# First loads on one queue and a held transposing load, in a gated attention and SwiGLU kernel

## Chip, cores, metric

One core of one Trainium2 chip. The metric is the device time of one execution in microseconds (us), median of several runs. All runs quoted here are undisturbed ("fast").

## The reference, cut

```python
def reference(A_x, A_wqkv, A_wo, B_x, B_w1, B_w3, B_w2, gate_w):
    x = A_x                                   # 1 x 2048 x 512, bf16
    g = sigmoid((x * gate_w).sum(-1, keepdims=True))
    # a: linear attention, 32 heads of 16; phi(t) = where(t > 0, t + 1, exp(t)) + 1e-6
    #    q, k, v from x @ wqkv; kv = phi(k)^T v; z = sum of phi(k); (phi(q) kv) / (phi(q) z) @ wo
    # b: (silu(x @ w1) * (x @ w3)) @ w2, hidden size 1376
    return g * a + (1 - g) * b
```

## The kernel before

Only the head matters: the first 10 us, in which TensorE (PE) warms up on constants, then transposes the first four token tiles of x itself and multiplies them with wk, while the rest of x arrives by transposing loads. PE's order is fixed by hand.

```python
dq = nc.sync
x_pairs = x2d[0:TB, :].rearrange("(g p j) d -> g p j d", p=P, j=2)      # TB = 512, P = 128
dq.dma_start(out=x_sb[:, 0:2, :], in_=x_pairs[0])                                   # "x pair 0"
nc.scalar.dma_start(out=wk_sb[:, 0:2, :], in_=wqkv_r[:, 0:2, D : 2 * D])            # "wk half 0"
dq.dma_start(out=wk_sb[:, 2:4, :], in_=wqkv_r[:, 2:4, D : 2 * D])                   # "wk half 1"
dq.dma_start(out=x_sb[:, 2:TPB, :], in_=x_pairs[1])                                 # "x pair 1"
pre = consts.tile([1, 1], FP32, name="pre")
nc.scalar.activation(out=pre[:], in_=..., func=ACT.Exp)     # loads the table early
for tb in range(1, NTB):
    dq.dma_start(out=xT[:, :, tb * TB : (tb + 1) * TB],     # transposing load
                 in_=x2d[tb * TB : (tb + 1) * TB, :], transpose=True)
    dq.dma_start(out=x_sb[:, tb * TPB : (tb + 1) * TPB, :], in_=x_r[:, ...])
# ... all other weights on dq; two Pool memsets of hr (128x512), 
# ... then PE in program order:
emit_warm(TB, TB, TB, TB, TB, TB, P, P, P)    # matmuls on constants
emit_xT(0); emit_xT(1)                        # PE transposes of x pair 0, copied to xT by DVE and ACT
for kc, t in ((0, 0), (1, 0), (0, 1), (1, 1), (2, 0), (3, 0)):   # four with wk half 0, two with half 1
    emit_k_mm(k0[t], t, kc)
emit_xT(2); emit_xT(3)                        # needs x pair 1
# ... ten more k matmuls, then per token tile t from 4: XP matmuls of tile t-4, k matmuls of tile t
#     (the first reader of a transposing load is token tile 4)
```

Of the kernel before, what the change touches and what calls it, by code (L numbers as in the profile page):

```python
# [11 lines left out]
ENG = mybir.EngineType  # L12
FP32 = mybir.dt.float32
BF16 = mybir.dt.bfloat16
# [3 lines left out]
def kernel(  # L18
# [12 lines left out]
    nc = tc.nc  # L31
    P = nc.NUM_PARTITIONS

    Bb, S, D = A_x.shape
    F = B_w1.shape[1]
# [3 lines left out]
    NT = S // P  # L39
    TB = 512  # L40
    NTB = S // TB
    TPB = TB // P
    FC = F // P
    FR = F - FC * P
    FM = FC * P
    NR = 2 * FR + 1
    HPC = P // Dh

    x2d = A_x.flatten_outer_dims()
    out2d = out.flatten_outer_dims()  # L50

    consts = ctx.enter_context(tc.tile_pool(name="consts", bufs=1))
# [11 lines left out]
    x_sb = consts.tile([P, NT, D], BF16, name="x_sb")  # L64
    xT = consts.tile([P, KC, S], BF16, name="xT")
    wk_sb = consts.tile([P, KC, D], BF16, name="wk_sb")
    wq_sb = consts.tile([P, KC, D], BF16, name="wq_sb")
    wv_sb = consts.tile([P, KC, D], BF16, name="wv_sb")
    w1_sb = consts.tile([P, KC, FM], BF16, name="w1_sb")
    w3_sb = consts.tile([P, KC, FM], BF16, name="w3_sb")  # L70
    wr_sb = consts.tile([P, KC, NR], BF16, name="wr_sb")
    w2_sb = consts.tile([P, FC, D], BF16, name="w2_sb")
    w2r_sb = consts.tile([P, D], BF16, name="w2r_sb")
    wo_sb = consts.tile([P, KC, D], BF16, name="wo_sb")

    wqkv_r = A_wqkv.rearrange("(kc d) n -> d kc n", d=P)
    w1_r = B_w1.rearrange("(kc d) f -> d kc f", d=P)
    w3_r = B_w3.rearrange("(kc d) f -> d kc f", d=P)
    x_r = x2d.rearrange("(t p) d -> p t d", p=P)
    dq = nc.sync  # L80
    x_pairs = x2d[0:TB, :].rearrange("(g p j) d -> g p j d", p=P, j=2)
    out_pairs = out2d[0:TB, :].rearrange("(g p j) d -> g j p d", p=P, j=2)
    dq.dma_start(out=x_sb[:, 0:2, :], in_=x_pairs[0])
    nc.scalar.dma_start(out=wk_sb[:, 0:2, :], in_=wqkv_r[:, 0:2, D : 2 * D])
    dq.dma_start(out=wk_sb[:, 2:4, :], in_=wqkv_r[:, 2:4, D : 2 * D])
    dq.dma_start(out=x_sb[:, 2:TPB, :], in_=x_pairs[1])
    pre = consts.tile([1, 1], FP32, name="pre")
    nc.scalar.activation(out=pre[:], in_=nc.const_aps.tensor(0.0, [1, 1], FP32), func=ACT.Exp)
    for tb in range(1, NTB):
        dq.dma_start(  # L90
            out=xT[:, :, tb * TB : (tb + 1) * TB], in_=x2d[tb * TB : (tb + 1) * TB, :],
            transpose=True,
        )
        dq.dma_start(
            out=x_sb[:, tb * TPB : (tb + 1) * TPB, :], in_=x_r[:, tb * TPB : (tb + 1) * TPB, :]
        )
    dq.dma_start(out=wq_sb[:], in_=wqkv_r[:, :, 0:D])
    dq.dma_start(out=wr_sb[:, :, 0:FR], in_=w1_r[:, :, FM:F])
    dq.dma_start(out=wr_sb[:, :, FR : 2 * FR], in_=w3_r[:, :, FM:F])
    with nc.allow_non_contiguous_dma(reason="one gate weight per partition and chunk"):  # L100
        dq.dma_start(
            out=wr_sb[:, :, 2 * FR : NR], in_=gate_w.rearrange("(kc d o) -> d kc o", d=P, o=1)
        )
    dq.dma_start(out=wv_sb[:], in_=wqkv_r[:, :, 2 * D : 3 * D])
    for fsl in (slice(0, FM // 2), slice(FM // 2, FM)):
        dq.dma_start(out=w1_sb[:, :, fsl], in_=w1_r[:, :, fsl])
        dq.dma_start(out=w3_sb[:, :, fsl], in_=w3_r[:, :, fsl])
    dq.dma_start(out=wo_sb[:], in_=A_wo.rearrange("(kc d) n -> d kc n", d=P))
    w2_r = B_w2[0:FM, :].rearrange("(fc f) d -> f fc d", f=P)
    for fcs in (slice(0, FC // 2), slice(FC // 2, FC)):  # L110
        dq.dma_start(out=w2_sb[:, fcs, :], in_=w2_r[:, fcs, :])
    dq.dma_start(out=w2r_sb[:FR, :], in_=B_w2[FM:F, :])

    pk_sb = consts.tile([P, NT, D], BF16, name="pk_sb")
    pks = consts.tile([P, D], FP32, name="pks")
    blockmask = consts.tile([P, P], FP32, name="blockmask")
    bm = blockmask[:].rearrange("p (b j) -> p b j", j=Dh)
    nc.gpsimd.memset(blockmask[:], 1.0)
# [1 line left out]
        out=bm, in_=bm, pattern=[[-Dh, HPC], [0, Dh]], compare_op=ALU.is_ge, fill=0.0,  # L120
# [3 lines left out]
        out=bm, in_=bm, pattern=[[Dh, HPC], [0, Dh]], compare_op=ALU.is_ge, fill=0.0,  # L124
        base=Dh - 1, channel_multiplier=-1,
    )
    XP_sb = consts.tile([P, KC, D], BF16, name="XP_sb")
    kvT_sb = consts.tile([P, KC, P], BF16, name="kvT_sb")
    W_sb = consts.tile([P, KC, D], BF16, name="W_sb")
    z_sb = consts.tile([P, D], FP32, name="z_sb")  # L130
    omg = consts.tile([P, NT], FP32, name="omg")
    hr_bufs = []
    for i in range(2):
        hrb = consts.tile([P, TPB, P], BF16, name=f"hr{i}")
        nc.gpsimd.memset(hrb[:], 0.0)
        hr_bufs.append(hrb)

    def phi(dst, ps):
        e = work.tile([P, D], BF16, tag="phi_e", name="phi_e")
        e_ins = nc.scalar.activation(out=e[:], in_=ps, func=ACT.Exp)  # L140
        em = work.tile([P, D], BF16, tag="phi_m", name="phi_m")
        nc.vector.tensor_scalar(  # L142
            out=em[:], in0=e[:], scalar1=1.0, scalar2=1e-6, op0=ALU.min, op1=ALU.add
        )
        nc.vector.scalar_tensor_tensor(  # L145
            out=dst, in0=ps, scalar=0.0, in1=em[:], op0=ALU.max, op1=ALU.add
        )
        return e_ins
# [259 lines left out]
    for c in range(KC):  # L408
# [7 lines left out]
        out=kvT_sb[:], in0=kvT_ps[:],  # L416
# [70 lines left out]
```

## Time and profile before

| | before |
|---|---|
| time, median of the first 3 runs | 180.26 us (180.18 to 180.34) |
| span of the profiled run | 178.7 us |
| PE busy | 97% |
| PE's share of the chain that ended last | 97% |

The page, its busy times by engine and its chain that ended last:

```profile
PE 174.1 (97%) x877; PEld 84.6 (47%) x893; DVE 119.3 (67%) x205; ACT 66.6 (37%) x126; POOL 61.3 (34%) x69
...
PE 97%; issue 1%; DVE 0%; DVEq 0%
```

PE is the bound, and nearly everything that ended late was PE itself. The head of PE, from the timeline (start us, duration us, engine, line, operation, out<-in, shape, count; a bracket names an idle time and what ended it):

```profile
0.84 3.04 PE L161 MATMUL warm<-const-bfloat16-1.0 128*128 128x512 bf16 x9 [0.84 <-PEq L471]
3.68 1.05 PE L174 MATMUL xTp<-ident,x_sb 128*128 128x128 bf16 x8
4.53 2.01 PE L184 MATMUL k<-wk_sb,xT 128*128 128x512 bf16 x6
6.37 0.61 PE L174 MATMUL xTp<-ident,x_sb 128*128 128x128 bf16 x8
6.82 2.32 PE L184 MATMUL k<-wk_sb,xT 128*128 128x512 bf16 x10
8.98 1.03 PE L204 MATMUL XP<-pk_sb,x_sb 128*128 128x512 bf16 x4
9.84 1.03 PE L184 MATMUL k_ps<-wk_sb,xT 128*128 128x512 bf16 x4
```

No bracket after the first line: PE never sits idle in this stretch. The first eight transposes start 0.11 us apart and the second eight 0.055, so somewhere in the six k matmuls PE's pace doubles. The Trainium skill (TensorE: Matmul & The Clock Gate, Part 1) gives 106.7 ns for the cold and 55.6 ns for the warm array at 128 columns; the trace agrees. The trace's record of the granted clock puts this **release** at 5.63 us. (The page's clock row shows full speed from the start, because it has no record for the time before the first release. The pace of the matmuls is what to read.)

The loads, from SyncE's (SP's) timeline, and then x pair 1 by its source line:

```profile
0.80 0.39 SPq L83 DMA_DIRECT2D x_sb<-in_A_x_dram  x1
1.26 0.41 SPq L85 DMA_DIRECT2D wk_sb<-in_A_wqkv_dram  x1
1.72 0.46 SPq L86 DMA_DIRECT2D x_sb<-in_A_x_dram  x1
2.23 3.49 SPq L90 DMA_TRANSPOSE xT<-in_A_x_dram  x1
```

```profile
L86 SPq DMA_DIRECT2D x_sb<-in_A_x_dram x1: 459/459/459, 1.7 to 1.7; - x1
...
DMA to landing us min/median/max: 4.2/4.2/4.2
```

The second number of a load's row is the time that SP takes to issue it. x pair 1 is issued at 1.72 us and has landed 4.2 us later, at 5.95; PE's second transposes started at 6.37. That is a slack of 0.4 us.

### The profile page before, as it was taken

What the parts mean: (1) busy time and instruction counts of PE and PEld (TensorE: products, weight loads), DVE (VectorE), ACT (ScalarE), POOL (GpSimd) and SP (SyncE); (2) the same over time, 40 slices, a digit from 0 to 9 for tenths busy, and PEclk for the clock granted to TensorE, in tenths of its full rate; (3) what the DMA queues carried; (4) which work ended last, traced back from release to release, by engine and by line L of the source; (5) the groups of instructions that cost most, each with busy time, mean ns of one, the idle gap of its engine ahead of it and who ended that gap; (6) DMA issues with size and microseconds to landing.
All of it is one profiled execution on the core that took longest, in us unless ns stands there. A gap on an engine that the chain in (4) does not pass through costs nothing.

```text
span 178.7 us, 2472 instructions
## 1 busy us (share of the span) xinstructions
PE 174.1 (97%) x877; PEld 84.6 (47%) x893; DVE 119.3 (67%) x205; ACT 66.6 (37%) x126; POOL 61.3 (34%) x69
## 2 busy tenths in 40 slices
PE   8999999999999999999999999999999999999993
PEld 4444444474444545444454544444545444444463
DVE  1588867997998837398786375978754669776000
ACT  3642323476533333342433333342433323341221
POOL 5187575736353323262003232620032328100000
PEclk9999999999999999999999999999999999999999
DMA  5999999901005010124000111240001023300011
GB/s 178 263 272 245 267 321 369 321 6 28 9 12 107 0 48 29 44 55 92 0 4 6 38 37 37 59 93 2 0 7 59 14 62 64 61 0 0 29 44 50
DMA packets 29085, 14.88 MB, mean 83 GB/s; under 512 B 19632, under 2 KB 28816, under 8 KB 29072
## 3 DMA queue, kind: packets, MB, share of 16 engines
q1 hardware_dynamic: 28800, 14.46, 30.2%
q10 hardware_dynamic: 272, 0.26, 0.5%
q8 instruction: 7, 0.11, 0.3%
q14 instruction: 6, 0.05, 0.1%
HBM read 8.42 MB, written 2.10 MB: 59 GB/s over the span
## 4 chain that ended last, share of the span: by engine, by line
PE 97%; issue 1%; DVE 0%; DVEq 0%
PE o_ps L355 19%; PE gate_ps L310 19%; PE up_ps L318 19%; PE o_ps L346 8%; PE q_ps L217 8%; PE XP L204 8%; PE k_ps L184 6%; PE r_ps L241 3%; PE k L184 2%; PE o_ps L350 2%; PE warm L161 2%; PE xTp L174 1%; PE kvT_ps L411 1%; PE W_ps L438 0%; DVE o_out L364 0%
## 5 line engine op out<-in xcount | busy, mean ns | idle before, releaser
L310 PE MATMUL gate_ps<-xT,w_sb 128*128 128x512 bf16 x156 | 40.7, 379 | 0.2
L318 PE MATMUL up_ps<-xT,w_sb 128*128 128x512 bf16 x156 | 40.5, 379 | 0.2
L225 POOL TENSOR_TENSOR qz<-pq,z_sb 128x512 f32<-128x512 bf16 x16 | 18.5, 1165 | 60.3 <-DVE pq L145 58.4
L323 ACT ACTIVATE th<-gate_ps 128x512 bf16<-128x512 f32 x40 | 23.9, 597 | 38.1 <-PE gate_ps L310 36.6
L355 PE MATMUL o_ps<-w_sb,hT 128*128 128x512 bf16 (+2 forms) x176 | 37.3, 354 | 0.2
L325 DVE SCALAR_TENSOR_TENSOR gs<-th,gate_ps 128x512 bf16<-128x512 bf16 x40 | 27.3, 684 | 5.8 <-ACT th L323 5.3
L328 DVE TENSOR_TENSOR hT<-up_ps,gs 128x512 bf16<-128x512 f32 x40 | 27.6, 691 | 3.8
L142 DVE TENSOR_SCALAR phi_m<-phi_e 128x512 bf16<-128x512 bf16 x32 | 15.2, 475 | 18.9 <-ACT phi_e L140 18.8
L355 PEld LDWEIGHTS <-hT 128*128 128x128 bf16 x180 | 16.8, 97 | 17.9
L318 PEld LDWEIGHTS <-w_sb 128*128 128x128 bf16 x160 | 15.6, 98 | 18.9
L310 PEld LDWEIGHTS <-w_sb 128*128 128x128 bf16 x160 | 15.6, 98 | 18.7
L360 ACT ACTIVATE o_out<-o_ps,omg 128x512 bf16<-128x512 f32 (+2 forms) x17 | 11.2, 656 | 30.4 <-PE o_ps L355 30.4
L290 POOL TENSOR_TENSOR pqn<-pq,rden 128x512 bf16<-128x512 bf16 x16 | 16.6, 1057 | 14.0 <-DVE rden L283 11.7
L194 POOL TENSOR_TENSOR pks<-pks,pk_sb 128x512 f32<-128x512 f32 x15 | 17.3, 1155 | 8.1 <-DVE pk_sb L145 7.5
L228 DVE TENSOR_REDUCE den<-qz 128x32 f32<-128x512 f32 x16 | 11.0, 684 | 9.0 <-POOL qz L225 8.9
L346 PE MATMUL o_ps<-W_sb,pqT 128*128 128x512 bf16 (+2 forms) x71 | 16.5, 355 | 0.1
L217 PE MATMUL q_ps<-wq_sb,xT 128*128 128x512 bf16 x63 | 16.4, 379 | 0.1
L204 PE MATMUL XP<-pk_sb,x_sb 128*128 128x512 bf16 x62 | 16.0, 379 | 0.1
L140 ACT ACTIVATE phi_e<-k_ps 128x512 bf16<-128x512 f32 x12 | 7.2, 597 | 14.4 <-PE k_ps L184 12.2
L140 ACT ACTIVATE phi_e<-q_ps 128x512 bf16<-128x512 f32 x16 | 9.6, 597 | 7.8 <-PE q_ps L217 6.7
L184 PE MATMUL k_ps<-wk_sb,xT 128*128 128x512 bf16 x48 | 12.3, 379 | 0.1
L145 DVE SCALAR_TENSOR_TENSOR pq<-q_ps,phi_m 128x512 bf16<-128x512 f32 x16 | 11.1, 691 | 0.5
(59 smaller groups left out, 119.5 us busy)
## 6 DMA issues: line engine op xcount, KB each, us to landing
w_sb<-in_B_w_dram SPq DMA_DIRECT2D x6, 640.0 KB, 8.5
out_dram<-o_out SPq DMA_DIRECT2D x15, 128.0 KB, 1.7
x_sb<-in_A_x_dram SPq DMA_DIRECT2D x3, 512.0 KB, 4.4
x_sb<-in_A_x_dram SPq DMA_DIRECT2D x2, 256.0 KB, 3.5
wq_sb<-in_A_wqkv_dram SPq DMA_DIRECT2D x1, 512.0 KB, 6.6
wv_sb<-in_A_wqkv_dram SPq DMA_DIRECT2D x1, 512.0 KB, 6.5
wo_sb<-in_A_wo_dram SPq DMA_DIRECT2D x1, 512.0 KB, 9.5
wk_sb<-in_A_wqkv_dram ACTq DMA_DIRECT2D x1, 256.0 KB, 3.7
```

The costliest lines, as they stand in the source:

```text
L184: nc.tensor.matmul(k_ps[:], lhsT=xT[:, kc, t * P : (t + 1) * P], rhs=wk_sb[:, kc, :], start=(kc == 0), stop=(kc == KC - 1),)
L194: nc.gpsimd.tensor_add(pks[:], pks[:], pk_sb[:, t, :])
L204: nc.tensor.matmul(XP_ps[dc][:], lhsT=x_sb[:, t, dc * P : (dc + 1) * P], rhs=pk_sb[:, t, :], start=(t == 0), stop=(t == NT - 1),)
L217: nc.tensor.matmul(q_ps[:], lhsT=xT[:, kc, ts_tok], rhs=wq_sb[:, kc, :], start=(kc == 0), stop=(kc == KC - 1),)
L225: nc.gpsimd.tensor_tensor(out=qz[:], in0=st[tb, "pq"][:, tt, :], in1=z_sb[:], op=ALU.mult)
L310: nc.tensor.matmul(gate_ps[:], lhsT=w1_sb[:, kc, fsl], rhs=xT[:, kc, tok_sl], start=(kc == 0), stop=(kc == KC - 1),)
L318: nc.tensor.matmul(up_ps[:], lhsT=w3_sb[:, kc, fsl], rhs=xT[:, kc, tok_sl], start=(kc == 0), stop=(kc == KC - 1),)
L323: nc.scalar.activation(out=th[:], in_=gate_ps[:], func=ACT.Tanh, scale=0.5)
L325: nc.vector.scalar_tensor_tensor(out=gs[:], in0=th[:], scalar=1.0, in1=gate_ps[:], op0=ALU.add, op1=ALU.mult)
L328: nc.vector.tensor_tensor(out=st[tb, "hT"][:, fc, :], in0=up_ps[:], in1=gs[:], op=ALU.mult)
L346: nc.tensor.matmul(o_ps[:], lhsT=st[tb, "pqT"][:, c, tsl], rhs=W_sb[:, c, a:b], start=(c == 0), stop=False,)
L355: nc.tensor.matmul(o_ps[:], lhsT=st[tb, "hT"][:, fc, tsl], rhs=w2_sb[:, fc, a:b], start=False, stop=(fc == FC - 1),)
```

## The change

The intent: put the four first loads on one queue, in the order in which PE needs them, and keep the big transposing load out of their way until they flow. A Pool memset of part of its target holds it (the load has to wait for the write to its target). So that SP keeps this order, its loads are put under a manual schedule; the other moved lines only make room for it.

```diff
     dq.dma_start(out=x_sb[:, 0:2, :], in_=x_pairs[0])
-    nc.scalar.dma_start(out=wk_sb[:, 0:2, :], in_=wqkv_r[:, 0:2, D : 2 * D])
+    dq.dma_start(out=wk_sb[:, 0:2, :], in_=wqkv_r[:, 0:2, D : 2 * D])
     dq.dma_start(out=wk_sb[:, 2:4, :], in_=wqkv_r[:, 2:4, D : 2 * D])
     dq.dma_start(out=x_sb[:, 2:TPB, :], in_=x_pairs[1])
 ...
+    # (blockmask and hr set-up moved up, before the loads)
+    nc.gpsimd.memset(xT[:, 0:3, TB : 2 * TB], 0.0)
+    with tc.manual_schedule(engines={ENG.SP}):
         for tb in range(1, NTB):
             dq.dma_start(out=xT[:, :, tb * TB : (tb + 1) * TB], ..., transpose=True)
 ... (the same loads in the same order)
```

## The prediction

> **What bounds the kernel.** TensorE. The page shows it busy 97% of the 178.7 us span, and the chain that ended last is 97% PE. In the timeline PE starts at 0.84 us. Nine warm-up matmuls on constants hold it until 3.68 us, the x transposes follow, and the first k matmul starts at 4.53 us. Start-to-start times are 0.11 us (128 columns) and 0.43 us (512 columns) up to about 5.7 us, then 0.055 and 0.216 us. The Trainium skill (TensorE: Matmul & The Clock Gate, Part 1) gives these as the back-to-back pace of a cold and a warm array: the trace agrees, so there is no gap between 3.68 and 10 us. First-load latency is already hidden.
>
> **What is removed, added, moved.** The four first loads (256 KB each) now all queue on SP. Landings before, from the tile views: x pair 0 at 0.80+2.8=3.6 us (used at 3.67), wk half 0 at 0.80+3.7=4.5 (used at 4.53), wk half 1 at 1.26+3.9=5.2 (used at about 5.9), x pair 1 at 1.72+4.2=5.9 (used at 6.16). After, wk half 0 is issued one SP issue (about 0.45 us) later, but behind x pair 0 alone instead of interleaved with it and with wk half 1. "Issuing engines are not separate DMA queues" (the Trainium skill, DMA: Bandwidth & Descriptors): the bytes ahead of it are no more, so I expect (estimates) landings near 3.3, 4.2, 4.8 and 5.5 us. PE, held by its warm-up matmuls, can use none of that.
>
> The first transposing load moves from 2.23 us to the end of the new Pool memset. Pool's last set-up memset ends at 3.00 us. Pool memsets took 0.20 us for 128 and 0.53 us for 512 elements per partition, so 1536 elements are about 1.4 us (estimate): it ends near 4.45, and the load is issued near 4.5. The three such loads landed 5.4 to 5.8 us after issue, of which 3.4 to 3.7 us is issue time, so it lands near 9.9 us instead of 7.7. Its first reader, the k matmuls of token tile 4, loads weights at 9.63 us. The slack of 1.9 us turns into a stall of about 0.3 us, which PE cannot win back.
>
> Everything behind it on SP moves 2.3 us later. Slack there is larger: second transposing load lands near 14.2 (needed about 16.5), wq near 23.7 (needed 30.3), w1 first half near 28.5 (needed 38.9).
>
> **Sum.** 180.26 - 0.0 (earlier first loads, off the path) + 0.3 (stall before tile 4), about 180.5 us, range 180.0 to 181.1. Chances: faster by over 2% 0.01, within 2% 0.97, slower 0.02.
>
> **What would show it.** Warm-up, transposes and the first k matmul at the same times (3.68, 4.53); first-load landings earlier; the Pool memset ending near 4.5 us; the transposing load landing near 9.9; a PE gap of 0.1 to 0.7 us just before the k matmuls of tile 4, and none later.
>
> **What would make it wrong.** The memset runs earlier on Pool or faster: then no stall, and the time equals before. The transposing load, no longer overlapping the first loads, is issued faster than 3.5 us: also none. One queue fills the DMA engines more slowly than two: wk half 0 lands after 4.5 us, and PE waits there. If unprofiled runs wait for wk half 0, which lands with almost no slack, a gain of some 0.1 us is possible.

## More of the kernel before

The end of the program, as ACT's sequencer sees it (line 482 is the closing barrier):

```profile
L482 ACTq DRAIN  x2: 14/206/398, 175.0 to 178.2; - x2
L482 ACTq EVENT_SEMAPHORE  x2: 17/17/17, 178.2 to 178.6; - x2
```

It passes two barriers, at 178.2 and 178.6 us, and its last drain takes 14 ns.

## The result

| | before | changed |
|---|---|---|
| time, median of 6 runs | 180.28 us (180.18 to 180.48) | 180.88 us (180.79 to 181.14) |
| ratio | | 1.0034 (1.0021 to 1.0047) |
| span of the profiled run | 178.68 us | 179.07 us |
| release of the clock | 5.63 us | 6.04 us |
| x pair 0 / wk half 0 landed | 3.63 / 4.47 us | 3.52 / 4.29 us |
| wk half 1 / x pair 1 landed | 5.20 / 5.95 us | 5.37 / 6.01 us |
| first transposing load: issue, landed | 2.23 + 3.49, 7.76 us | 4.34 + 2.01, 8.63 us |
| last DVE write to end of span | 2.45 us | 2.64 us |

A ratio is the mean time of one kernel's fast runs over that of the other's of the same rounds, so it isn't quite the ratio of the medians. Figures with two decimals that the views round to one are taken from the trace's records. The time is inside the predicted range. The reason given for it is another matter. PE's timeline after the change:

```profile
0.84 3.04 PE L161 MATMUL warm<-const-bfloat16-1.0 128*128 128x512 bf16 x9 [0.84 <-PEq L471]
3.67 1.06 PE L174 MATMUL xTp<-ident,x_sb 128*128 128x128 bf16 x8
4.53 2.21 PE L184 MATMUL k<-wk_sb,xT 128*128 128x512 bf16 x6
6.57 0.61 PE L174 MATMUL xTp<-ident,x_sb 128*128 128x128 bf16 x8
7.02 2.32 PE L184 MATMUL k<-wk_sb,xT 128*128 128x512 bf16 x10
9.18 1.03 PE L204 MATMUL XP<-pk_sb,x_sb 128*128 128x512 bf16 x4
10.04 1.03 PE L184 MATMUL k_ps<-wk_sb,xT 128*128 128x512 bf16 x4
```

There is no gap in front of the k matmuls of token tile 4 (the last line): the stall that was predicted there doesn't exist. PE is 0.20 us later from the second transposes on, because the six k matmuls took 2.21 us instead of 2.01: the clock was released 0.41 us later, and at half pace that costs half of it. From there to the end, every weight load of the two traces has this same distance of 0.20 us. SP's timeline, x pair 1, and ACT's end:

```profile
0.80 0.39 SPq L83 DMA_DIRECT2D x_sb<-in_A_x_dram  x1
1.26 0.42 SPq L84 DMA_DIRECT2D wk_sb<-in_A_wqkv_dram  x1
1.72 0.46 SPq L85 DMA_DIRECT2D wk_sb<-in_A_wqkv_dram  x1
2.23 0.47 SPq L86 DMA_DIRECT2D x_sb<-in_A_x_dram  x1
4.34 2.01 SPq L108 DMA_TRANSPOSE xT<-in_A_x_dram  x1
```

```profile
L86 SPq DMA_DIRECT2D x_sb<-in_A_x_dram x1: 468/468/468, 2.2 to 2.2; - x1
...
DMA to landing us min/median/max: 3.8/3.8/3.8
```

```profile
L482 ACTq DRAIN  x2: 127/262/397, 175.2 to 178.7; - x2
L482 ACTq EVENT_SEMAPHORE  x2: 17/17/17, 178.4 to 179.0; - x2
```

The transposing load is issued when predicted but in 2.01 us instead of 3.5, so it lands well before its need. ACT's last drain starts 0.36 us after the barrier instead of 0.07 and takes 127 ns instead of 14, and the last barrier comes 0.67 us after the one before it, not 0.47. So this pair of traces differs by 0.20 (release) + 0.19 (tail) = 0.39 us, which is the whole difference of the spans.

That raises two questions. Does the change make the release late, or is that chance? And what are the other 0.2 us of the 0.6 that the timed runs show?

### The profile page after: what moved, and what is told of

It reads as the page before. It is cut to its first block, busy times and chain, and to the rows that moved or that the text cites. A ratio compares the mean times of both kernels' runs of the same rounds, so it can differ in the third digit from the quotient of the medians.

```text
span 179.1 us, 2490 instructions
## 1 busy us (share of the span) xinstructions
PE 175.1 (98%) x893; PEld 84.8 (47%) x893; DVE 119.3 (67%) x205; ACT 66.6 (37%) x126; POOL 62.6 (35%) x70
## 4 chain that ended last, share of the span: by engine, by line
PE 98%; DVE 0%; issue 0%; DVEq 0%
PE o_ps L355 19%; PE gate_ps L310 19%; PE up_ps L318 19%; PE o_ps L346 8%; PE q_ps L217 8%; PE XP L204 8%; PE k_ps L184 6%; PE r_ps L241 3%; PE k L184 2%; PE o_ps L350 2%; PE warm L161 2%; PE xTp L174 1%; PE kvT_ps L411 0%; PE W_ps L438 0%; DVE o_out L364 0%; PE z_ps L429 0%
## 5 line engine op out<-in xcount | busy, mean ns | idle before, releaser
L318 PE MATMUL up_ps<-xT,w_sb 128*128 128x512 bf16 x160 | 41.1, 379 | 0.0
```

Of the source, the lines that this page charges most:

```text
L318: nc.tensor.matmul(up_ps[:], lhsT=w3_sb[:, kc, fsl], rhs=xT[:, kc, tok_sl], start=(kc == 0), stop=(kc == KC - 1),)
```

## The experiments

Twelve kernels on three chips, four per call, each with the kernel before timed beside it on the same chip (11 runs of it a call). All gave correct results.

### e1_act_queue: wk half 0 back on ACT, the hold stays

```diff
-    dq.dma_start(out=wk_sb[:, 0:2, :], ...)
+    nc.scalar.dma_start(out=wk_sb[:, 0:2, :], ...)     # in the changed kernel
```

> The changed kernel with one thing undone: wk half 0 goes back to ACT's queue (the Pool hold stays). Theory A (the +0.6 us comes from ACT's stream having one instruction and one DMA queue less: the clock is released later after the first instruction, 6.04 us against 5.63, and the last drain of ACT comes 0.4 us late): time within 0.15 us of the kernel before (180.3), clock release near 5.6 us, last DVE write to span end near 2.45 us. Theory B (the late transposing load and all later loads cost the time): time stays near 180.9. Theory C (release time and tail are chance of the single profiles): release anywhere, time undetermined.

180.52 us (179.96 to 181.11) against 180.35; ratio 1.0007 (0.9986 to 1.0027). Release 5.72 us, tail 2.44 us; wk half 1 landed at 5.07 and x pair 1 at 5.69 us. So the hold by itself costs nothing that shows, and brings x pair 1 forward by 0.26 us against the profile before. Nor do the manual schedule and the moved lines, which e1 keeps. That points to the move of one load to SP as what costs, though the two intervals still overlap a little (up to 1.0027 here, from 1.0021 for the change). Theory A fits so far.

### e2_no_hold: the queue move alone

```diff
-    nc.gpsimd.memset(xT[:, 0:3, TB : 2 * TB], 0.0)
```

> The changed kernel without the Pool memset: all four first loads on SP, the transposing load right behind them. Theory A: time stays near 180.9 us (ratio to before about 1.003), release near 6.0, late ACT drain still there, since ACT's stream is that of the changed kernel. Theory B: time falls to 180.3. Both: the first transposing load, overlapping the first loads again, needs about 3.5 us to issue (2.0 us when held).

181.26 us, ratio 1.0044 (1.0026 to 1.0062): no theory had expected it above the changed kernel, but the intervals of the two overlap. The tail is 2.63 us as A expected, but the release is early, 4.89 us. PE's timeline shows why that didn't help:

```profile
6.04 0.59 PE L183 MATMUL k<-wk_sb,xT 128*128 128x512 bf16 x2 [0.31 <-DMA wk_sb<-in_A_wqkv_dram]
7.24 0.62 PE L173 MATMUL xTp<-ident,x_sb 128*128 128x128 bf16 x8 [0.60 <-DMA x_sb<-in_A_x_dram]
```

PE waits for first loads: wk half 1 landed at 6.00 and x pair 1 at 7.19 us. This is the load conflict that the hold was made for: right behind the others on the same queue, the transposing load delays x pair 1. It took 4.25 us to issue; the prediction's 3.4 to 3.7 us were such values too: in the profile before, each of the three transposing loads was issued more than 3 us before the load ahead of it landed.

### e3_act_pad: one more instruction in ACT's stream

```diff
     nc.scalar.activation(out=pre[:], ..., func=ACT.Exp)
+    nc.scalar.activation(out=pre2[:], ..., func=ACT.Exp)
```

> The changed kernel with one more 1x1 activation on ACT right behind the first one, so that ACT's stream has as many instructions as in the kernel before, but no DMA queue. Theory A1 (the late last drain is an instruction fetch whose place is set by ACT's instruction count): the tail after the last DVE write falls from 2.64 to 2.45 us, so 180.7; if the release too follows the stream's length, 180.3. Theory A2 (both follow from the missing ACT DMA queue): no change, 180.9.

180.91 us, ratio 1.0025 (1.0012 to 1.0039). ACT's end in this trace:

```profile
L484 ACTq DRAIN  x2: 14/206/399, 175.5 to 178.8; - x2
L484 ACTq EVENT_SEMAPHORE  x2: 17/17/17, 178.7 to 179.2; - x2
```

The drain takes 14 ns again and the tail is 2.44 us: A1 is right about the tail. The release was at 6.69 us, so it doesn't follow the stream's length.

### e4_tiny_act_dma: a 1 KB load on ACT that nobody needs

```diff
+    scrap = consts.tile([1, D], BF16, name="scrap")
+    nc.scalar.dma_start(out=scrap[:], in_=gate_w.rearrange("(o d) -> o d", o=1))
```

> The changed kernel plus a 1 KB load on ACT's queue into a tile that nobody reads; the first loads and the hold stay as changed. Theory A: time near 180.3 us, release near 5.6 us, tail 2.45 us, as in the kernel before, though no data that matter move on ACT's queue. Theory B: 180.9.

181.07 us, ratio 1.0042 (1.0028 to 1.0056), release 6.71, tail 2.55 us. Having an ACT queue does not bring the release forward: theory A falls, apart from the tail. (The last drain takes 14 ns here too. The other 0.1 us lies before the first barrier, which comes 2.02 us after the last DVE write and 1.89 to 1.92 in all other traces; what delays it was not followed up.)

### f1_before_again and f2_changed_again: the two kernels once more, on one chip

> The kernel before, unchanged, as a run of its own. In the runs so far, apart from the one without a hold, the last weight load came at 172.70 us + half the release time, to 0.03 us. Theory D (the moment of release belongs to the launch and scatters from kernel to kernel and run to run, whatever the change): release anywhere between 4.8 and 6.8 us, last weight load at 172.70 + half of it, tail 2.45 us, time within 0.2% of before. Theory E (loads order sets the release): release near 5.6.

180.26 us, ratio 0.9991 (0.9971 to 1.0011); release 5.22, tail 2.44 us.

> The changed kernel again. Theory D: release anywhere between 4.8 and 6.8 us, tail 2.64 us; time 180.3 + 0.19 (tail) + half of the difference in release, so 180.3 to 181.1. Theory E: release 6.0 to 6.7 us again, +0.5 to +0.7 us over before.

180.91 us, ratio 1.0028 (1.0008 to 1.0048); tail 2.64 us. The cost is there again, but the release was at **4.71 us**, earlier than in any trace of the kernel before, so the order of the loads doesn't make it late: theory E falls, and what D expected of an early release (a time near 180.3) did not come either. PE's timeline and what it waited for in the first 20 us:

```profile
4.54 1.12 PE L184 MATMUL k<-wk_sb,xT 128*128 128x512 bf16 x4
6.07 0.59 PE L184 MATMUL k<-wk_sb,xT 128*128 128x512 bf16 x2 [0.41 <-DMA wk_sb<-in_A_wqkv_dram]
6.72 0.62 PE L174 MATMUL xTp<-ident,x_sb 128*128 128x128 bf16 x8
...
10.20 1.03 PE L184 MATMUL k_ps<-wk_sb,xT 128*128 128x512 bf16 x4
```

```profile
PE warm L161 <- PEq L471: 0.8, 1, 0.8
PE k L184 <- DMA wk_sb<-in_A_wqkv_dram: 0.4, 1, 0.4
```

```profile
L86 SPq DMA_DIRECT2D x_sb<-in_A_x_dram x1: 467/467/467, 2.2 to 2.2; - x1
...
  PEld L174: 0.6, 1
...
DMA to landing us min/median/max: 4.4/4.4/4.4
```

The four k matmuls with wk half 0 run warm after the first and are done early; then PE waits for wk half 1 (landed 6.03), and the weight load of the second transposes waits for x pair 1 (landed 6.67). This is a new theory, **F: in the changed kernel the last two first loads land later, and PE waits for them whenever the clock is released early.**

### f3_placebo_act and f4_placebo_pool: changes that touch no load

```diff
+    nc.scalar.activation(out=pre2[:], ..., func=ACT.Exp)          # f3, in the kernel before
+    nc.gpsimd.memset(scrap[:], 0.0)                               # f4, 128x1536, nobody waits
```

> The kernel before with one more 1x1 activation that nobody reads (its ACT stream is one longer, 195). Theory D: the release may shift by as much as in the changed kernel although no load moved, +-0.5 us of time. Theory E: time as before within 0.15 us, release near 5.6. Tail 2.45 us in both[...].

180.60 us, ratio 1.0004 (0.9984 to 1.0024); release 6.36, tail 2.44 us.

> The kernel before with the 128x1536 Pool memset aimed at a tile nobody reads and nothing waits for. Theory D: release may shift, +-0.5 us of time. Theory E: as before within 0.15 us. If the Pool memset itself cost anything (a rival nobody has shown), it would show here as a time above before at the same release.

180.26 us, ratio 0.9991 (0.9967 to 1.0015); release 5.29, tail 2.45 us. The memset costs nothing. Neither placebo moves the time by what D allowed: the release scatters from run to run, and no kernel was shown to have a release of its own.

### g1_before_long_warm and g2_changed_long_warm: PE asks for the loads later

```diff
-    emit_warm(TB, TB, TB, TB, TB, TB, P, P, P)
+    emit_warm(TB, TB, TB, TB, TB, TB, TB, TB, TB, TB, P, P, P)
```

> The kernel before with four more 512-column warm-up matmuls, so that PE asks for every first load 0.9 to 1.7 us later. Both theories: no first load is waited for any more; time 180.3 + 0.9 to 1.7 us, about 181.6. It is the partner of the next run.

181.30 us, ratio to before 1.0045 (1.0032 to 1.0059); tail 2.43 us.

> The changed kernel with the same four more warm-up matmuls. Theory F (the changed kernel's +0.6 us is 0.19 us of tail, plus wk half 1 and x pair 1 that land 0.2 to 0.8 us later and are waited for whenever the clock is released early): nothing is waited for here, so it is 0.2 us over its long-warm partner, within the 0.3 us that the scatter of the release leaves. Theory E (the loads' order makes the release late): +0.5 to +0.7 us over its partner still. The first transposing load lands near 9.0 us, needed near 11: no wait.

181.69 us, ratio to before 1.0065 (1.0050 to 1.0080); tail 2.64 us. In neither trace does PE wait for a load in the head. The distance of the pair is 0.39 us: inside F's 0.2 +- 0.3 and below E's 0.5, but a difference of two medians with this scatter is a weak witness. The traces are the stronger ones.

### g3_long_hold: the hold three times as long

```diff
-    nc.gpsimd.memset(xT[:, 0:3, TB : 2 * TB], 0.0)
+    nc.gpsimd.memset(xT[:, 0:3, TB : 2 * TB], 0.0)     # three times
```

> The changed kernel with the Pool memset three times over: the transposing load is issued near 7.1 us instead of 4.34. If the slack in front of token tile 4 is as read (it lands 4.3 to 5.0 us after issue, needed at 9.8 to 10.2 us), it lands at 11.2 to 12 and PE stalls 1.2 to 2.0 us just before those k matmuls; time 182.1 to 182.9. This is the stall that the prediction expected of the change itself. If instead the transposing load was what delayed x pair 1, that pair lands below 6.0 us here; if the loads delay each other, it lands at 6.0 to 6.7 as in the changed kernel.

182.28 us (182.22 to 182.31), ratio 1.0102 (1.0089 to 1.0115). PE's timeline:

```profile
6.13 0.59 PE L186 MATMUL k<-wk_sb,xT 128*128 128x512 bf16 x2 [0.71 <-DMA wk_sb<-in_A_wqkv_dram]
6.77 0.62 PE L176 MATMUL xTp<-ident,x_sb 128*128 128x128 bf16 x8
...
11.51 1.02 PE L186 MATMUL k_ps<-wk_sb,xT 128*128 128x512 bf16 x4 [1.09 <-DMA xT<-in_A_x_dram]
```

Here is the stall that the prediction expected of the change itself. The load was issued at 7.21 us, in 2.06 us, and landed at 11.37; tile 4 starts 4.74 us after the second transposes instead of 3.47, so the stall costs 1.3 us. And with nothing at all behind them, wk half 1 still landed at 6.09 and x pair 1 at 6.72 us: it is not the transposing load that makes them late in the changed kernel. The release was at 3.76 us, the earliest of all traces, and PE could use none of it.

### g4_x1_on_act: x pair 1 on ACT instead

```diff
-    dq.dma_start(out=x_sb[:, 2:TPB, :], in_=x_pairs[1])
     nc.scalar.activation(out=pre[:], ..., func=ACT.Exp)
+    nc.scalar.dma_start(out=x_sb[:, 2:TPB, :], in_=x_pairs[1])
```

> The changed kernel with x pair 1 on ACT's queue behind the first activation, so that it is issued near 2.3 us, as late as on SP. ACT's stream is then as long as in the kernel before: tail 2.45 us. Theory F1 (x pair 1 is late because one queue serves all four): it lands below 5.8 us, early releases pay again, time within 0.15 us of before (180.3). Theory F2 (it is late because it is issued late and stands behind 768 KB): it lands at 6.0 to 6.7 us, time 180.5 to 180.8.

180.42 us, ratio 1.0001 (0.9987 to 1.0015), tail 2.45 us. The experiment missed its aim: in this trace ACT's sequencer didn't wait for its engine's table load (0.80 to 2.08 us), so x pair 1 was issued at 0.86 us, not at 2.3, and F1 and F2 aren't told apart. It shows something else: it crowds wk half 0 (landed 4.95, and PE began its k matmuls at 4.99 instead of 4.53), but all four loads have landed by 5.59 us, and no cost of the change is left to see.

### All heads in one table

Where nothing but the clock limits it, the start of the second transposes is 3.55 us plus half the release. All in us, from the traces; the last column but one is the later of wk half 1 and x pair 1.

| kernel | first loads on | release | 3.55 + half of it | last first load landed | second transposes start |
|---|---|---|---|---|---|
| before | SP, one ACT | 5.63 | 6.37 | 5.95 | 6.37 |
| f1_before_again | SP, one ACT | 5.22 | 6.16 | 5.98 | 6.17 |
| f3_placebo_act | SP, one ACT | 6.36 | 6.73 | 6.08 | 6.73 |
| f4_placebo_pool | SP, one ACT | 5.29 | 6.20 | 6.00 | 6.21 |
| e1_act_queue | SP, one ACT | 5.72 | 6.41 | 5.69 | 6.42 |
| g4_x1_on_act | SP, one ACT | 5.39 | 6.24 | 5.59 | 6.46 (waited for wk half 0) |
| changed | SP | 6.04 | 6.57 | 6.01 | 6.57 |
| e3_act_pad | SP | 6.69 | 6.90 | 6.43 | 6.91 |
| e4_tiny_act_dma | SP | 6.71 | 6.90 | 6.72 | 6.90 |
| f2_changed_again | SP | 4.71 | 5.91 | 6.67 | **6.72** |
| g3_long_hold | SP | 3.76 | 5.43 | 6.72 | **6.77** |
| e2_no_hold | SP | 4.89 | 5.99 | 7.19 | **7.24** |

From the second transposes to PE's last weight load it is 169.14 us, to 0.01, in every trace but that of g3 (1.26 more). So the span is 169.14 us after the later of two things, the clock's path and the last first load + 0.05 us, plus what follows the last weight load. With one load on ACT the loads come last in none of these traces; with all on SP they come last in three of six, those with an early release. The release itself is no different between the groups: with the long-warm pair, its mean is 5.55 us in 7 traces with one first load on ACT and 5.57 in 7 with all on SP.

An estimate of the terms: take the 14 releases with each of the landings of the kernels whose loads are as before (5.95, 5.98, 6.08, 6.00 and g1's 6.18) and with each of those with all on SP and a hold (6.01, 6.43, 6.72, 6.67, 6.72 and g2's 6.87). The mean of the later path is 6.40 us in the first case and 6.70 in the second, so 0.30 us. With 0.20 us of tail that makes 0.5; measured were 0.62 (means of the first result) and 0.51 (f2). The rest may be the scatter of the release. It also stays unsettled why e3, whose tail is mended, measured 0.49 and e4 0.77 over before.

The timed runs are a second witness, because the record has the span and the mean granted clock of each. The full-clock record lasted 174.08 us in 13 of the 14 traces. So a mean below 1 says that it ended before the span did, and hence that the release was early. Seven of the 39 runs of the kernel before (f1 among them) have such a mean, and their spans are 178.4 to 178.6 us. Worked back from the mean (an estimate), they were released at 3.4 to 4.0 us, and the clock's path alone (3.55 us, half the release, 169.14, and 3.17 after the last weight load, 3.35 with the change) would give spans of 177.6 to 177.9. Three of the twelve runs of the changed kernel have it, with spans of 179.2 to 179.6 us, where releases of 3.9 to 5.3 us would give 178.0 to 178.7. So at an early release both kernels wait for their first loads, and the changed one is 0.6 to 1.2 us longer, of which the tail is only 0.2. This is what F says, now also from runs without a trace here (one of the three is f2's). It means too that the kernel before is not free of such waits, though its traces show none. In the long-warm pair four of five runs without the change and two of six with it have a mean below 1, so some of their 0.39 us is chance.

Why do the two loads land later? Each is issued one SP issue (0.5 us) later, and the traces show one thing more. From 3.5 to 5.0 us all four loads had been issued (the last by 2.70 us), yet less data moved. The last two numbers of a row are the busy share of the DMA engines and GB/s, first for e1, then for the changed kernel:

```profile
3.50:5.00 1.50, 1.50 (x14) 1.13 (x13) 0.58 (x2) 0.61 (x2) 0.80 (x1) 1.00 1.09 395
3.50:5.00 1.50, 1.50 (x14) 1.21 (x13) 0.58 (x2) 0.62 (x2) 0.81 (x1) 1.00 1.08 325
```

In this stretch it was 344 to 395 GB/s in the seven traces with one first load on ACT, and 206 to 337 in the seven with all on SP. Whether the single queue or the later issue lowers the rate is not shown.

## Why the prediction was right or wrong

- **Right: the bound, and the size class.** PE bound, first-load latency hidden in the profiled run of the kernel before, a cost of a few tenths, no gain. 180.88 us lies in 180.0 to 181.1.
- **Wrong: the stall of 0.3 us before token tile 4.** The step was "of which 3.4 to 3.7 us is issue time, so it lands near 9.9 us". That issue time belonged to loads issued into a busy queue (3.49 us before, 4.25 in e2): in these two traces and the four others without a hold, the issue ended 0.16 to 0.24 us before x pair 1, the load ahead, had landed. Held back, it was 1.9 to 2.6 us, and the load landed at 8.4 to 9.3 us, about 0.7 us or more ahead of its need. The mechanism exists (g3: 1.3 us) but the hold of the change is too short for it. The prediction named a faster issue among the things that would make it wrong.
- **Right: the memset.** Estimated to end near 4.45 us; it took 1.38 us and ended at 4.31. It costs the kernel nothing that shows (f4).
- **Wrong: "landings near 3.3, 4.2, 4.8 and 5.5 us. PE, held by its warm-up matmuls, can use none of that."** The first two are right to about 0.2 us (3.52 and 4.29 in the changed kernel). The last two measured 5.37 to 6.08 and 6.01 to 6.72 us in the four traces of the changed kernel's loads and short hold (changed, e3, e4, f2); before, they were 5.20 and 5.95. The prediction counted only the bytes ahead of a load, and took the rate at which they move for unchanged (it was lower, 206 to 337 GB/s for 344 to 395). "One queue fills the DMA engines more slowly than two" does stand among the things that would make it wrong, but for wk half 0, which wasn't late. It overlooked that wk half 1 and x pair 1 move back by one issue of SP too (1.26 to 1.72 and 1.72 to 2.23 us), and that x pair 1 had little slack (0.4 us in the profile before). It also took the one profile's release as the kernel's: with an earlier release, PE asks for them sooner. This is the estimated 0.30 us.
- **Missing: any term for the end of the program.** The prediction's sum has none. ACT's stream is one instruction shorter without its load, 193 for 194 in the trace, and that costs 0.19 us after PE's last work. All five traces with 193 (changed, e2, f2, g2, g3) have a tail of 2.61 to 2.65 us, all with 194 or 195 but e4 have 2.43 to 2.45; e3 turns it off with one idle activation. The likely cause is the fetch of ACT's next instructions: an 8 KiB packet on an instruction queue starts at 176.4 us in the kernel before, while SP is still issuing the last store, and at 179.4 us in the changed one, after the span. In all five traces with 193 it starts 2.9 to 3.0 us after the last DVE write, in those with 194 it starts 0.15 to 0.45 after it. By the records, that packet is too late to be what the drain waited for, so this cause is only argued; that the length of the stream decides is shown.
- So the right time was luck. It came from a wrong sum: 0.3 us of a stall that doesn't exist, in place of 0.2 us of tail and about 0.3 us of late first loads.

No version beats the kernel before by more than the scatter; e1 and g4 equal it.

## What to carry to other kernels

Before loads are moved, list the slack of each of them against the earliest time at which its reader can want it, over several traces, not in one: a clock that is released at 3.8 us in one run and 6.7 in another moves the need by 1.5 us. The issue time of a load here depended on the queue that it was issued into, so don't carry it to a place where the queue is empty. And when a time moves by 0.3%, compare the traces' last microseconds too: an instruction less on an idle engine cost a third of the difference here.

## What the Trainium skill lacked or had wrong

- TensorE: Matmul & The Clock Gate, Part 1: the transition "varies ±500ns". In 14 traces it came between 3.76 and 6.71 us, with PE starting at 0.84 in all of them: a spread of 2.95 us, about the 3.4 us of the window that the page names. The page also calls the count of cold matmuls run-variable, and this fits better. So does the window: the full-clock record lasts 174.08 us in 13 traces and 177.49 in g3, which is 51 and 52 times 3.413. The page gives no figure for the scatter that follows from run to run: here it is half of the spread, 1.5 us of 180, where no load is waited for.
- DMA: Bandwidth & Descriptors, Issuing engines are not separate DMA queues: issuing on several engines saves only the sequencer's time, "usually small relative to the DMA itself". In this head it was not small: with the changed kernel's hold, moving one 256 KB load from ACT to SP moved x pair 1 from 5.69 (e1) to 6.01 to 6.72 us. Its own issue came 0.5 us later (2.23 for 1.73 us). The data rate from 3.5 to 5.0 us was lower too (206 to 337 GB/s for 344 to 395 with one load on ACT). Whether that follows from the later issue or from the single queue, no run told apart.
- DMA: Bandwidth & Descriptors doesn't say that the time to issue a transposing load depends on what is in flight: for the first one here it took 1.9 to 2.6 us when issued with two of the four first loads landed, 2.06 with all landed (g3), and 3.5 to 4.3 with none.
- Runtime: NRT & Kernel Launch, Instruction fetch mechanics: refills are said to be 16 KiB and mostly hidden. One instruction queue here moved 16 KiB packets, the other 8 KiB ones, and a stream one instruction shorter than before cost 0.19 us at the end of the program. That a refill is the cause is not shown.
